# Spectral filter beside a gated MLP: background work tied one product later, and an eight-point butterfly in another order

## The chip, the cores and the metric

The kernel runs on one core of one Trainium2 chip. The metric is the time of one execution in device microseconds. Before the change it is 444.45 us, the median of three runs (443.97 to 444.93).

The core has five engines that run side by side, each through its own list of instructions in a fixed order: TensorE (PE), VectorE (DVE), ScalarE (ACT), GpSimd (POOL) and SyncE (SP), which starts the DMAs. An instruction waits at the head of its engine's list until the semaphores that it needs have been raised, and everything behind it waits too.

## The reference

The input is normalized by rows, and three things are summed: the input itself, a filter in the frequency domain (a two-dimensional FFT over sequence and features, a product with complex weights, the FFT back) and a gated MLP.

```python
# S, D, F = 2048, 448, 1792
def _A_ref(x, w_r, w_i):
    X = rfft2(x, axes=(-2, -1))
    X = X * (w_r + 1j * w_i)
    return irfft2(X, s=(S, D), axes=(-2, -1))

def _B_ref(x, W_gate, W_up, W_down):
    gate = jnp.einsum("bsd,df->bsf", x, W_gate)
    up = jnp.einsum("bsd,df->bsf", x, W_up)
    gate = gate * (gate > 0)
    return jnp.einsum("bsf,fd->bsd", gate * up, W_down)

x = A_x
xn = _layernorm(x, axis=-1)
return x + _A_ref(xn, A_w_r, A_w_i) + _B_ref(xn, B_W_gate, B_W_up, B_W_down)
```

## The kernel before

**The MLP is the foreground.** Every fp32 operand is split into two fp16 parts, a high and a low one, and each product is three matmuls (high by high, high by low, low by high). The 14 blocks of 128 hidden features stand in groups of 5, 5 and 4; the 2048 rows in four chunks of 512 (`CHUNKS`). A *gate/up unit* (`gu_unit`) multiplies one chunk by one block into two PSUM banks `gu`: 20 full matmuls of 512 columns in `gu_full`, and half matmuls in `gu_halves` that two units share. Its *product* (`gu_post`) is a chain over two engines: `gu_relu` on ACT (L887), `gu_times` on DVE (L891), `gu_hi` on ACT (L895), `gu_lo` on DVE (L899). The bank is free for a later unit when L891 has read it. A *down unit* (`dn_mm`, L923) multiplies 128 rows by a whole group into a bank that ACT presets with the running sum (`dn_seed`) and reads back (`dn_post`).

**The filter is the background.** It is a list `bg` of small steps, each with a cost in DVE time. Forward, for each of eight indices: `f_dft` (matmuls L417), an eight-point butterfly `f_a` and `f_b` on DVE over a tile `eo` with a scratch tile `bw`, a split (`f_hi` on ACT, `f_lo` on DVE L443), `f_sdft` (matmuls L450), then butterflies over sequence indices. In the middle the product with the weights. Inverse, for each index p of 0 to 7: `i_join` (DVE L678, L679) fills a tile `U[p]`; `i_swap` has SP copy its two partition halves crosswise into a tile `sw` by DMA; `i_pair` (L604, L605) adds them; `i_mix` runs the eight-point butterfly between `U[p]` and a scratch tile; `i_hi` (ACT L710) and `i_lo` (DVE, two L715) split the result into `vt`; `i_sdft` (matmuls L723) multiplies it into a bank `fx`; `i_pqhi` (ACT L729) and `i_pqlo` (DVE L732) split that into `wf` and free the bank; `i_ddft` (matmuls L753) makes 128-row blocks of output, in banks which ACT presets (L743) and reads back (L759), or, where a down unit holds the same rows, without a preset (`two_banks`) and with an addition on DVE (`i_acc`). U tiles, scratch tiles and weight tiles of the MLP share four buffers named `wst`, so their rows carry this name in a profile; `y` are the tiles of the butterflies over sequence indices, whose rotations are the pairs L458, L459 and L462, L463.

**What sets the order.** The opening (up to some 34 us) is written out by hand. Behind it, each unit issues its matmuls, then as many background steps as its share of DVE time pays for (`run_bg`, `room`), and then its product. The share is the same factor for all units, found so that the list ends `LASTGU` gate/up units before the last. A list scheduler then places all instructions on the engines by dependences, priorities and its own estimate of the time. `after(LAG)` binds every background step of a unit behind the last DVE and ACT instructions of an earlier product: `anchors` holds L891 and L887 of each unit so far (of a down unit its `dn_post`), and `LAG` says how many units back it reaches from the one just before.

The butterfly `eight_a`, `eight_b`, `turn` works on rows of 58 numbers, 16 rows to a tile (8 by real and imaginary part). Where an instruction reads or overwrites what an earlier DVE instruction touched, it carries a wait for that one.

Of the kernel before, what the change touches and what calls it, by code (L numbers as in the profile page):

```python
# [10 lines left out]
F32 = mybir.dt.float32  # L11
# [15 lines left out]
N2ORD = [0, 8, 4, 12, 2, 10, 6, 14, 1, 9, 5, 13, 3, 11, 7, 15]
CHUNKS = [0, 2, 1, 3]
# [12 lines left out]
"""  # L41
EXPMASK = 0x7F800000
EXPONE = float(1 << 23)
LASTGU = 9
SQ = 2.0 ** -16


# [96 lines left out]
def tile_gfnet_reglu(ctx: ExitStack, tc: tile.TileContext, x, xr, wgu, wd, wf, ident, c_fd, c_fm, c_im, c_row, c_id,  # L144
                     out):
    nc = tc.nc
    V, A, P, G = nc.vector, nc.scalar, nc.tensor, nc.gpsimd
# [4 lines left out]
    def mt(shape, dt, name, bufs=1):  # L152
        return main.tile(shape, dt, name=name, bufs=bufs)
# [65 lines left out]
    def load_xr(n2):  # L219
# [2 lines left out]
        xr_t[n2] = xr_b[n2].rearrange("p g c k -> p (g c k)")[:, 0:D]  # L222
        nc.sync.dma_start(xr_t[n2], xrv[:, n2, :])

    wst, wdst, fm_t, im_t, wf_t = {}, {}, {}, {}, {}

    def load_w(f, g, eng=nc.sync):
        if g == 0:
            t = mt([128, 2, 4, 128], F32, "wst", 4)
            wst[f, 0], wst[f, 1] = t[:, 0], t[:, 1]  # L230
        eng.dma_start(wst[f, g], wgu[f, :, g])

# [141 lines left out]

    def turn(o, a, b, u, v, sgn):

        o2 = o.rearrange("p l c k -> p (l c) k")
        x, y = slice(2 * a, 2 * b + 2, 2 * (b - a) + 1), slice(2 * b, 2 * a, 2 * (a - b) + 1)
        p, m = (OP.add, OP.subtract) if sgn > 0 else (OP.subtract, OP.add)
        V.tensor_tensor(o2[:, x], u, v[:, ::-1], op=p)  # L380
        V.tensor_tensor(o2[:, y], u, v[:, ::-1], op=m)

    def eight_b(X, w, s, sgn):

        turn(w, 4, 5, w[:, 3], w[:, 7], sgn)
        turn(w, 6, 7, w[:, 2], s[:, 2], sgn)
        V.tensor_tensor(X[:, 0], s[:, 0], s[:, 1], op=OP.add)
        V.tensor_tensor(X[:, 4], s[:, 0], s[:, 1], op=OP.subtract)
        turn(X, 2, 6, w[:, 0], w[:, 1], sgn)
        V.scalar_tensor_tensor(X[:, 1:8:6], w[:, 6:8], RT, w[:, 4:6], op0=OP.mult, op1=OP.add)  # L390
# [61 lines left out]
    def rotate(t, b, p, sgn):  # L452

        th = 2 * np.pi * p / 16
        c, s = float(np.cos(th)), float(np.sin(th)) * sgn
        if abs(c) >= abs(s) - 1e-9:
            k, f = s / c, c
            V.scalar_tensor_tensor(t[:, :, 0], b[:, :, 1], k, b[:, :, 0], op0=OP.mult, op1=OP.add)  # L458
            V.scalar_tensor_tensor(t[:, :, 1], b[:, :, 0], -k, b[:, :, 1], op0=OP.mult, op1=OP.add)  # L459
        else:  # L460
            k, f = c / s, s
            V.scalar_tensor_tensor(t[:, :, 0], b[:, :, 0], k, b[:, :, 1], op0=OP.mult, op1=OP.add)  # L462
            V.scalar_tensor_tensor(t[:, :, 1], b[:, :, 1], k, b[:, :, 0], op0=OP.mult, op1=OP.subtract)  # L463
        return f
# [195 lines left out]
    U = {}  # L660

    def i_join(p):

        u = U[p] = mt([128, 2, 4, 128], F32, "wst", 4).rearrange("p a b c -> p (a b c)")[:, 0:2 * XW].rearrange(
            "p (g c k) -> p g c k", g=NG, c=2)
        a, b = cur.pop(("i3", 0, p)), cur.pop(("i3", 1, p))
        o, d = (u[:, :, :, KC * i:KC * (i + 1)] for i in range(2))
        if p == 0:
            V.tensor_tensor(o, a, b, op=OP.add)
            V.tensor_tensor(d, a, b, op=OP.subtract)  # L670
        elif p == 4:
            for x, o1, o2 in ((o, OP.subtract, OP.add), (d, OP.add, OP.subtract)):
                V.tensor_tensor(x[:, :, 0], a[:, :, 0], b[:, :, 1], op=o1)
                V.tensor_tensor(x[:, :, 1], a[:, :, 1], b[:, :, 0], op=o2)
        else:
            t = free.pop(0)
            f = rotate(t, b, p, -1)
            V.scalar_tensor_tensor(o, t, f, a, op0=OP.mult, op1=OP.add)  # L678
            V.scalar_tensor_tensor(d, t, -f, a, op0=OP.mult, op1=OP.add)  # L679
            free.append(t)  # L680
        free.extend((a, b))
# [287 lines left out]
    def add(cost, fn, *a):  # L969
        bg.append((cost, PE_US.get(fn.__name__, 0.0), fn, a))  # L970
# [187 lines left out]
    for f in groups[1] + groups[2]:  # L1158
        s = first[f]
# [15 lines left out]
    for g, fs in enumerate(groups):  # L1175
        s = max(i for i in gus if i < first["dn", g])
# [192 lines left out]
```

## Time and profile before

| | |
|---|---|
| median of three runs | 444.45 us |
| profiled execution, whole | 444.21 us |
| its span, first to last instruction | 442.4 us |
| PE busy | 431.8 us, 3009 matmuls |
| DVE busy | 375.7 us, 922 instructions |
| ACT busy | 254.0 us |
| gate/up matmuls L852 | 1140, 255.8 us |
| down matmuls L923 | 624, 127.6 us |
| idle of DVE ahead of L891, ended by ACT's L887 | 18.4 us |
| idle of DVE ahead of L604, ended by the DMA of the swap | 5.1 us |

The profile comes from one execution with the hardware profiler. A row of a timeline has the start in us, the length, engine and line, the instruction, the tile written and the tiles read, shapes, how many instructions it merges, and in brackets how long the engine had been idle and what ended it. Instructions overlap at their ends, so the difference of two starts tells what one costs its engine. Engines other than PE may idle without cost, as long as PE doesn't wait for them.

### The profile page before, as it was taken

How to read it: one execution, taken by the hardware profiler on the slowest of the kernel's cores; microseconds unless marked ns; L12 is line 12 of the kernel's file. 1: busy time of each engine (PE TensorE's matmuls, PEld its weight loads, DVE VectorE, ACT ScalarE, POOL GpSimd, SP SyncE). 2: the span in 40 equal slices, each digit the busy share in tenths (PEclk: the TensorE clock that was granted, in tenths of full speed). 3: DMA queues.
4: the chain of work that ended last, by engine and by line, in shares of the span. 5: the costliest groups of instructions: out<-in, count | busy, mean ns of one | idle time of the engine just before them, and what ended most of it. 6: DMA issues, size and time to landing. Idle time of an engine off the chain costs nothing.

```text
span 442.4 us, 8132 instructions
## 1 busy us (share of the span) xinstructions
PE 431.8 (98%) x3009; PEld 209.9 (47%) x3009; DVE 375.7 (85%) x922; ACT 254.0 (57%) x515; POOL 39.7 (9%) x84
## 2 busy tenths in 40 slices
PE   6899999999999999999999999999999989999996
PEld 2543544454454444444444444444554544555544
DVE  5988798999988899999999998798989789974312
ACT  5888484587367837625425465664655653765530
POOL 2320030032300030000000041000000000000000
PEclk9999999999999999999999999999999999999999
DMA  7839995016000473522302100020201220120202
GB/s 251 296 92 243 382 296 103 2 32 77 3 0 2 144 219 120 164 85 65 107 1 85 42 1 1 2 85 1 89 10 56 77 74 17 63 76 7 105 22 83
DMA packets 38360, 39.66 MB, mean 90 GB/s; under 512 B 18592, under 2 KB 33216, under 8 KB 38320
## 3 DMA queue, kind: packets, MB, share of 16 engines
q1 hardware_dynamic: 38320, 39.14, 29.3%
q8 instruction: 23, 0.38, 0.4%
q14 instruction: 17, 0.14, 0.1%
HBM read 24.25 MB, written 3.67 MB: 63 GB/s over the span
## 4 chain that ended last, share of the span: by engine, by line
PE 76%; DVE 13%; DMA 6%; issue 1%; SPq 1%; ACT 0%; POOL 0%; DVEq 0%; ACTq 0%
PE gu L852 43%; PE dn L923 23%; DMA sw<-wst 3%; PE gu L859 3%; DMA wst<-in_wgu 2%; PE fx L450 2%; DVE vt L715 1%; PE fx L417 1%; DVE g L891 1%; PE fx L723 1%; DMA y<-in_xr 1%; DVE h L899 1%; PE dn L955 1%; DVE wst L604 1%; PE fx L753 1%
## 5 line engine op out<-in xcount | busy, mean ns | idle before, releaser
L852 PE MATMUL gu<-T,wt 128*128 128x512 f16 (+1 forms) x1140 | 255.8, 376 | 1.6 <-DVE g L891 1.2
L852 PEld LDWEIGHTS <-wt 128*128 128x128 f16 x1140 | 108.7, 98 | 132.4 <-issue 10.8
L923 PE MATMUL dn<-wdt,h 128*128 128x448 f16 x624 | 127.6, 353 | 0.0
L923 PEld LDWEIGHTS <-h 128*128 128x128 f16 x624 | 60.2, 98 | 57.0
L895 ACT ACTIVATE h<-g 128x512 f16<-128x512 f32 x56 | 34.9, 626 | 65.7 <-DVE g L891 65.6
L887 ACT ACTIVATE g<-gu 128x512 f32<-128x512 f32 x56 | 33.0, 589 | 38.5 <-PE gu L859 23.3
L891 DVE SCALAR_TENSOR_TENSOR g<-gu,g 128x512 f32<-128x512 f32 x56 | 38.4, 685 | 18.6 <-ACT g L887 18.4
L899 DVE TENSOR_TENSOR h<-g,h 128x512 f16<-128x512 f32 x56 | 38.3, 685 | 6.0 <-ACT h L895 6.0
L927 ACT ACTIVATE xy<-dn,dsc 128x448 f32<-128x448 f32 x44 | 27.6, 629 | 25.0 <-PE dn L923 24.9
L192 POOL PARTITION_ALL_REDUCE wm<-wm x15 | 16.0, 1072 | 155.8 <-ACT junk L189 155.8
L916 ACT ACTIVATE dn<-xy,dinv 128x448 f32<-128x448 f32 x44 | 27.6, 632 | 0.5
L805 DVE SCALAR_TENSOR_TENSOR wt<-wst,wsc,wt 128x512 f16<-128x512 f32 x28 | 20.6, 748 | 1.0 <-ACT wt L801 1.0
L801 ACT ACTIVATE wt<-wst,wsc 128x512 f16<-128x512 f32 x28 | 19.2, 713 | 1.8 <-DVE wsc L199 1.8
L189 ACT ACTIVATE junk<-wst 128x512 bf16<-128x512 f32 x28 | 17.4, 621 | 1.1 <-DMA wst<-in_wgu 0.9
L859 PE MATMUL gu<-T,wt 64*128 64x512 f16 x112 | 17.0, 381 | 0.1
L732 DVE SCALAR_TENSOR_TENSOR wf<-fx,wf 128x512 f16<-128x512 f32 x16 | 10.9, 688 | 4.9 <-ACT wf L729 4.9
L255 DVE BATCH_NORM_STATS2 bst<-y 128x6 f32<-128x448 f32 x16 | 9.6, 615 | 5.7 <-DMA y<-in_xr 5.7
L440 ACT ACTIVATE Xh<-eo 128x464 f16<-128x464 f32 x16 | 8.9, 596 | 8.7 <-DVE eo L391 8.7
L710 ACT ACTIVATE vt<-wst,fsc 128x928 f16<-128x928 f32 x8 | 8.8, 1097 | 8.6 <-DVE wst L391 6.1
L470 DVE TENSOR_TENSOR y<-y,y 128x464 f32<-128x464 f32 x21 | 13.4, 637 | 0.2
L471 DVE TENSOR_TENSOR y<-y,y 128x464 f32<-128x464 f32 x21 | 13.3, 636 | 0.0
L723 PEld LDWEIGHTS <-vt 128*128 128x128 f16 x192 | 11.4, 98 | 2.0 <-issue 0.4
(156 smaller groups left out, 506.8 us busy)
## 6 DMA issues: line engine op xcount, KB each, us to landing
wst<-in_wgu SPq DMA_DIRECT2D x28, 256.0 KB
wf<-in_wf SPq DMA_DIRECT2D x16, 232.0 KB
sw<-y SPq DMA_DIRECT2D x32, 114.2 KB
sw<-wst SPq DMA_DIRECT2D x16, 228.4 KB
y<-in_xr SPq DMA_DIRECT2D x16, 224.0 KB
xy<-in_x SPq DMA_DIRECT2D x16, 224.0 KB
out<-xy SPq DMA_DIRECT2D x15, 224.0 KB
wdst<-in_wd SPq DMA_DIRECT2D x14, 224.0 KB
```

What stands on the lines that cost most here:

```text
L189: A.activation(mt([128, 512], BF16, "junk")[:, 0:src.shape[-1]], src, AF.Square, scale=SQ, accum_out=acc)
L801: A.activation(w[:, 0:4, :], wst[f, g], AF.Copy, scale=wsc[f, g])
L805: V.scalar_tensor_tensor(w[:, 4:8, :], st, sc, w[:, 0:4, :], op0=OP.mult, op1=OP.subtract)
L852: last["P"] = P.matmul(hps[f, q][:, g, cs], wt[f, g][:, a, :], Tq[q][:, b, cs], start=(start and i == 0), stop=(stop and i == len(seq) - 1 ...
L859: m = P.matmul(hps[f, q][:, g, 0:512], wt[f, g][rows, 7, :], Tq[q][rows, b, :], start=start, stop=not start).ins
L887: last["A"] = A.activation(g1s[f, q], hps[f, q][:, 0, :], AF.Relu, scale=2.0 ** -22).ins
L891: last["V"] = V.scalar_tensor_tensor(g1, hps[f, q][:, 1, :], 2.0 ** -22, g1, op0=OP.mult, op1=OP.mult).ins
L895: A.activation(ht[f, q][:, 0, :], g1s[f, q], AF.Copy)
L899: V.tensor_tensor(h[:, 1, :], g1s.pop((f, q)), h[:, 0, :], op=OP.subtract)
L916: A.activation(dps[n2][:, 0:D], xy[n2], AF.Copy, scale=dinv[:, g:g + 1])
L923: last["P"] = P.matmul(dps[n2][:, 0:D], ht[f, q][:, a, js], wdt[f][:, b, :], start=False, stop=(f == fs[-1] and a == 1), skip_group_check= ...
L927: last["A"] = A.activation(xy[n2], dps[n2][:, 0:D], AF.Copy, scale=dsc[:, g:g + 1]).ins
```

## The change

Four things are changed; TensorE's, SP's and GpSimd's instructions are the same in number.

- `LAG` is 0 in place of 1: background steps of a unit are bound behind the product of the unit just before it, not the one before that.
- `LASTGU` is 11 in place of 9, so the background list ends two units earlier and each unit's share is larger. The costs of the forward butterfly's halves are 1.99 and 2.14 in place of 1.97 and 2.1.
- The tiles `wst` have 18 rows of 58 (1044 numbers) in place of 1024 numbers, and a butterfly takes the first 16 rows directly.
- The butterfly puts its second sums into rows 2, 4, 6 and its differences into rows 1, 3, 5 of the tile `F`, which leaves rows 0 to 2 of the scratch tile free for the next turn; `eight_b` takes the first sums ahead of the turns.

```diff
-LAG, AHEAD, RAMP = 1, 3, 6
+LAG, AHEAD, RAMP = 0, 3, 6
-LASTGU = 9
+LASTGU = 11
...
+    def wide():
+        return mt([128, 18, 2 * KC], F32, "wst", 4)
+
+    def eight_rows():
+        return wide()[:, 0:2 * NG].rearrange("p (g c) k -> p g c k", c=2)
...
-            t = mt([128, 2, 4, 128], F32, "wst", 4)
+            t = wide().rearrange("p a k -> p (a k)")[:, 0:1024].rearrange("p (g a b) -> p g a b", g=2, a=4)
...
-        V.tensor_tensor(s, w[:, 0:3], w[:, 4:7], op=OP.add)
-        V.tensor_tensor(w[:, 0:3], w[:, 0:3], w[:, 4:7], op=OP.subtract)
+        V.tensor_tensor(F[:, 2:7:2], w[:, 0:3], w[:, 4:7], op=OP.add)
+        V.tensor_tensor(F[:, 1:6:2], w[:, 0:3], w[:, 4:7], op=OP.subtract)
...
+        V.tensor_tensor(F[:, 0], F[:, 2], F[:, 4], op=OP.add)
+        V.tensor_tensor(F[:, 4], F[:, 2], F[:, 4], op=OP.subtract)
         turn(w, 4, 5, w[:, 3], w[:, 7], sgn)
-        turn(w, 6, 7, w[:, 2], s[:, 2], sgn)
-        V.tensor_tensor(X[:, 0], s[:, 0], s[:, 1], op=OP.add)
-        V.tensor_tensor(X[:, 4], s[:, 0], s[:, 1], op=OP.subtract)
-        turn(X, 2, 6, w[:, 0], w[:, 1], sgn)
-        V.scalar_tensor_tensor(X[:, 1:8:6], w[:, 6:8], RT, w[:, 4:6], op0=OP.mult, op1=OP.add)
-        V.scalar_tensor_tensor(X[:, 5:2:-2], w[:, 6:8], -RT, w[:, 4:6], op0=OP.mult, op1=OP.add)
+        turn(w, 0, 1, F[:, 5], F[:, 6], sgn)
+        turn(F, 2, 6, F[:, 1], F[:, 3], sgn)
+        V.scalar_tensor_tensor(F[:, 1:8:6], w[:, 0:2], RT, w[:, 4:6], op0=OP.mult, op1=OP.add)
+        V.scalar_tensor_tensor(F[:, 5:2:-2], w[:, 0:2], -RT, w[:, 4:6], op0=OP.mult, op1=OP.add)
...
-            state["mix"] = mt([128, 2, 4, 128], F32, "wst", 4).rearrange("p a b c -> p (a b c)")[:, 0:2 * XW].rearrange(
-                "p (g c k) -> p g c k", g=NG, c=2)
-            eight_a(u, state["mix"], u[:, 1:4])
+            state["mix"] = eight_rows()
+            eight_a(u, state["mix"])
...
-        add(1.97, f_a, a)
-        add(2.1, f_b, a)
+        add(1.99, f_a, a)
+        add(2.14, f_b, a)
```

The first two constants and the scheduler move instructions all over the program, so what stands where is shown at three places. In the changed kernel's rows a line number is 4 to 6 higher for the same instruction (L887 is L891, L891 is L895, L732 is L736, L380 is L386).

First the butterfly itself, on DVE: the first forward one, in tiles `eo` and `bw`, with the waits that its rows carry (`DVE` for a wait on an earlier DVE row). Before:

```order
L372 TENSOR_TENSOR eo<-bw 128x348 [waits DVE_49]
L373 TENSOR_TENSOR bw<-bw 128x348 [waits DVE_49]
L387 TENSOR_TENSOR eo<-eo 128x116
L388 TENSOR_TENSOR eo<-eo 128x116
L271 RECIPROCAL rs<-rs 128x4 [waits Activation_49]
L380 TENSOR_TENSOR bw<-bw 128x2x58 [waits DVE_49]
L381 TENSOR_TENSOR bw<-bw 128x2x58
L380 TENSOR_TENSOR eo<-bw 128x2x58 [waits DVE_49]
L381 TENSOR_TENSOR eo<-bw 128x2x58
```

After the change, the same place:

```order
L378 TENSOR_TENSOR eo<-bw 128x3x116 [waits DVE_49]
L379 TENSOR_TENSOR eo<-bw 128x3x116
L391 TENSOR_TENSOR eo<-eo 128x116 [waits DVE_49]
L386 TENSOR_TENSOR bw<-bw 128x2x58 [waits DVE_49]
L387 TENSOR_TENSOR bw<-bw 128x2x58
L386 TENSOR_TENSOR bw<-eo 128x2x58
L392 TENSOR_TENSOR eo<-eo 128x116 [waits DVE_49]
L387 TENSOR_TENSOR bw<-eo 128x2x58
L386 TENSOR_TENSOR eo<-eo 128x2x58 [waits DVE_49]
```

The second difference no longer waits for the row directly ahead, and most other waits are for rows two or more back. (In the inverse butterflies before, nearly each of these rows waited for the one ahead.)

Second, DVE where the last split of inverse index 3 stands (L732, `wf`, of which the second frees the bank that ACT presets for the matmuls L753). Before:

```order
L891 SCALAR_TENSOR_TENSOR g1_4537<-gu_4469,g1_4537 128x512
L604 TENSOR_TENSOR wst_4527<-wst_4527,sw0_2361 128x8x58
L605 TENSOR_TENSOR wst_4527<-wst_4527,sw0_2361 128x8x58
L380 TENSOR_TENSOR wst_4624<-wst_4624 128x2x58
L732 SCALAR_TENSOR_TENSOR wf_4348<-fx_4322,wf_4348 128x512
L715 SCALAR_TENSOR_TENSOR vt_2359<-wst_4169,fsc_88,vt_2359 128x16x29 x2
L732 SCALAR_TENSOR_TENSOR wf_4350<-fx_4335,wf_4350 128x512
L381 TENSOR_TENSOR wst_4624<-wst_4624 128x2x58
L899 TENSOR_TENSOR h_4540<-g1_4537,h_4540 128x512
L380 TENSOR_TENSOR wst_4624<-wst_4624,wst_4352 128x2x58
L891 SCALAR_TENSOR_TENSOR g1_4639<-gu_4490,g1_4639 128x512
```

After, from the pairing to the second split:

```order
L610 TENSOR_TENSOR wst_4500<-wst_4500,sw0_2270 128x8x58
L611 TENSOR_TENSOR wst_4500<-wst_4500,sw0_2270 128x8x58
L903 TENSOR_TENSOR h_4617<-g1_4614,h_4617 128x512
L378 TENSOR_TENSOR wst_4314<-wst_4569 128x3x116
L379 TENSOR_TENSOR wst_4314<-wst_4569 128x3x116
L736 SCALAR_TENSOR_TENSOR wf_4310<-fx_4284,wf_4310 128x512
L391 TENSOR_TENSOR wst_4314<-wst_4314 128x116
L719 SCALAR_TENSOR_TENSOR vt_2268<-wst_4137,fsc_88,vt_2268 128x16x29 x2
L386 TENSOR_TENSOR wst_4569<-wst_4569 128x2x58
L387 TENSOR_TENSOR wst_4569<-wst_4569 128x2x58
L386 TENSOR_TENSOR wst_4569<-wst_4314 128x2x58
L736 SCALAR_TENSOR_TENSOR wf_4312<-fx_4297,wf_4312 128x512
```

Between the pairing and the second split stand a low part of the MLP and six butterfly rows more; the next product (L895) follows seven rows behind it.

Third, ACT in the forward transform, at the first relu behind the opening (`g1_1038`). Before:

```order
L320 ACTIVATE tt1_102<-y15_81,rs_964 128x448
L320 ACTIVATE tt2_103<-y14_80,rs_964 128x448
L320 ACTIVATE tt3_104<-y0_66,rs_964 128x448
L927 ACTIVATE xy_61<-dn_847,dsc_91 128x448
L887 ACTIVATE g1_1038<-gu_979 128x512
L493 ACTIVATE y11_77<-fx_822 128x464
```

After:

```order
L931 ACTIVATE xy_61<-dn_847,dsc_91 128x448
L324 ACTIVATE y15_81<-y9_75,rs_964 128x448
L324 ACTIVATE y14_80<-y17_83,rs_964 128x448
L324 ACTIVATE y0_66<-y8_74,rs_964 128x448
L920 ACTIVATE dn_1433<-xy_61,dinv_92 128x448
L499 ACTIVATE y11_77<-fx_822 128x464
L326 ACTIVATE tt0_101<-y12_78,rs_964 128x448
L326 ACTIVATE tt1_102<-y15_81,rs_964 128x448
L446 ACTIVATE Xh_864<-eo_818 128x464
L446 ACTIVATE Xh_866<-eo_818 128x464
L326 ACTIVATE tt2_103<-y14_80,rs_964 128x448
L891 ACTIVATE g1_1038<-gu_979 128x512
```

The relu, which stood directly behind the read-back of the down unit (L927), now stands behind three normalizations, a preset, the evacuation L499 and five more rows.

More of the change, by code (lines that the diff above doesn't have):

```diff
@@ L363, in tile_gfnet_reglu, with eight_a @@
     RT = float(np.sqrt(0.5))
-    def eight_a(F, w, s):
+    def eight_a(F, w):
         f, p = (t.rearrange("p (h s) c k -> p h s (c k)", h=2) for t in (F[:, 0:8], w[:, 0:8]))
@@ L381, in turn, with eight_b @@
         V.tensor_tensor(o2[:, y], u, v[:, ::-1], op=m)
-    def eight_b(X, w, s, sgn):
+    def eight_b(F, w, sgn):
+        V.tensor_tensor(F[:, 0], F[:, 2], F[:, 4], op=OP.add)
+        V.tensor_tensor(F[:, 4], F[:, 2], F[:, 4], op=OP.subtract)
         turn(w, 4, 5, w[:, 3], w[:, 7], sgn)
-        turn(w, 6, 7, w[:, 2], s[:, 2], sgn)
-        V.tensor_tensor(X[:, 0], s[:, 0], s[:, 1], op=OP.add)
-        V.tensor_tensor(X[:, 4], s[:, 0], s[:, 1], op=OP.subtract)
-        turn(X, 2, 6, w[:, 0], w[:, 1], sgn)
-        V.scalar_tensor_tensor(X[:, 1:8:6], w[:, 6:8], RT, w[:, 4:6], op0=OP.mult, op1=OP.add)
-        V.scalar_tensor_tensor(X[:, 5:2:-2], w[:, 6:8], -RT, w[:, 4:6], op0=OP.mult, op1=OP.add)
+        turn(w, 0, 1, F[:, 5], F[:, 6], sgn)
+        turn(F, 2, 6, F[:, 1], F[:, 3], sgn)
+        V.scalar_tensor_tensor(F[:, 1:8:6], w[:, 0:2], RT, w[:, 4:6], op0=OP.mult, op1=OP.add)
+        V.scalar_tensor_tensor(F[:, 5:2:-2], w[:, 0:2], -RT, w[:, 4:6], op0=OP.mult, op1=OP.add)
     def chained(m, prev):
@@ L428, in f_a @@
         w = state["bw"] = ft([128, NG, 2, 2 * KC], F32, "bw")
-        eight_a(Fq[a], w, Fq[a][:, 1:4])
+        eight_a(Fq[a], w)
     def f_b(a):
-        eight_b(Fq[a], state["bw"], Fq[a][:, 1:4], 1)
+        eight_b(Fq[a], state["bw"], 1)
     def f_part(a, n2):
@@ L662, in i_join @@
     def i_join(p):
-        u = U[p] = mt([128, 2, 4, 128], F32, "wst", 4).rearrange("p a b c -> p (a b c)")[:, 0:2 * XW].rearrange(
-            "p (g c k) -> p g c k", g=NG, c=2)
+        u = U[p] = eight_rows()
         a, b = cur.pop(("i3", 0, p)), cur.pop(("i3", 1, p))
@@ L697, in i_mix @@
         if half == 0:
-            state["mix"] = mt([128, 2, 4, 128], F32, "wst", 4).rearrange("p a b c -> p (a b c)")[:, 0:2 * XW].rearrange(
-                "p (g c k) -> p g c k", g=NG, c=2)
-            eight_a(u, state["mix"], u[:, 1:4])
+            state["mix"] = eight_rows()
+            eight_a(u, state["mix"])
         else:
-            eight_b(u, state["mix"], u[:, 1:4], -1)
+            eight_b(u, state["mix"], -1)
     def i_sides(p):
```

## Prediction

> **What bounds the kernel now.** I read the page's first part, then TensorE's order in time, then the in-order queues of VectorE (DVE) and ScalarE (ACT) where TensorE stops.
>
> ```profile
> span 442.4 us, 8132 instructions
> PE 431.8 (98%) x3009; PEld 209.9 (47%) x3009; DVE 375.7 (85%) x922; ACT 254.0 (57%) x515; POOL 39.7 (9%) x84
> PE 76%; DVE 13%; DMA 6%; issue 1%; SPq 1%; ACT 0%; POOL 0%; DVEq 0%; ACTq 0%
> ```
>
> TensorE is busy for 431.8 of 442.4 us, and neither program gives it other work (3009 matmuls in both). A gain can come only from places where it stands still behind the warm-up; a loss comes from any new one. DVE holds 13% of the chain that ended last, so somewhere it sets the time. That place is the inverse transform:
>
> ```profile
> 312.00:371.00 59.00, 57.38 (x527) 29.89 (x525) 53.05 (x125) 33.30 (x57) 0.00 (x0) 1.00 0.18 58
> 371.00:437.00 66.00, 66.00 (x585) 35.28 (x582) 35.53 (x74) 33.48 (x57) 0.00 (x0) 1.00 0.14 48
> ...
> 305.36 0.60 PE L859 MATMUL gu<-T,wt 64*128 64x512 f16 x4
> 305.89 4.49 PE L852 MATMUL gu<-T,wt 128*128 128x512 f16 x20
> ...
> 362.75 0.54 PE L923 MATMUL dn<-wdt,h 128*128 128x448 f16 x2
> 364.48 4.48 PE L852 MATMUL gu<-T,wt 128*128 128x512 f16 x20 [1.19 <-DVE g L891]
> 368.79 0.73 PE L923 MATMUL dn<-wdt,h 128*128 128x448 f16 x3
> 369.84 0.80 PE L753 MATMUL fx<-idc_t,wf 64*128 64x56 f16 x48 [0.31 <-ACT fx L743]
> 370.74 0.61 PE L859 MATMUL gu<-T,wt 64*128 64x512 f16 x4
> ```
>
> The first two rows are stretches: length, then the busy time of PE, weight loads, DVE, ACT and GpSimd. DVE works 53 of 59 us in the first, 35.5 of 66 in the second. In the others, columns are start and length. By starts, 20 gate/up matmuls take 4.31 us (364.48 to 368.79), 0.216 each; I take 0.19 for a down matmul. So TensorE waits 1.73 - 2 x 0.19 = 1.35 us ahead of 364.48 for a product on DVE (L891), 1.05 - 3 x 0.19 = 0.48 us ahead of 369.84 for the preset of a bank by ACT (L743), and about 0.1 ahead of 370.74. Together 1.9 us: everything that the change could win in the middle of the kernel. Why DVE is late there:
>
> ```profile
> 306.69 0.69 DVE L891 SCALAR_TENSOR_TENSOR g<-gu,g 128x512 f32<-128x512 f32 x1 [1.72 <-ACT g L887]
> 309.02 1.31 DVE L715 SCALAR_TENSOR_TENSOR vt<-wst,fsc,vt 128x464 f16<-128x464 f32 x2
> 310.24 0.69 DVE L899 TENSOR_TENSOR h<-g,h 128x512 f16<-128x512 f32 x1
> ...
> 313.65 0.40 DVE L462 SCALAR_TENSOR_TENSOR y<-y 128x232 f32<-128x232 f32 x1
> 313.96 0.40 DVE L463 SCALAR_TENSOR_TENSOR y<-y 128x232 f32<-128x232 f32 x1
> ...
> 322.49 0.64 DVE L604 TENSOR_TENSOR wst<-wst,sw 128x464 f32<-128x464 f32 x1 [1.81 <-DMA sw<-wst]
> ...
> 331.38 0.27 DVE L387 TENSOR_TENSOR wst<-wst 128x116 f32<-128x116 f32 x1
> 331.57 0.27 DVE L388 TENSOR_TENSOR wst<-wst 128x116 f32<-128x116 f32 x1
> ...
> 347.54 0.64 DVE L679 SCALAR_TENSOR_TENSOR wst<-y,y 128x464 f32<-128x464 f32 x1
> 348.10 0.40 DVE L390 SCALAR_TENSOR_TENSOR wst<-wst 128x232 f32<-128x232 f32 x1
> ...
> 354.15 0.64 DVE L604 TENSOR_TENSOR wst<-wst,sw 128x464 f32<-128x464 f32 x1 [2.37 <-DMA sw<-wst]
> ...
> 357.85 0.64 DVE L679 SCALAR_TENSOR_TENSOR wst<-y,y 128x464 f32<-128x464 f32 x1
> 358.40 0.28 DVE L380 TENSOR_TENSOR wst<-wst 128x116 f32<-128x116 f32 x1
> 358.71 0.28 DVE L381 TENSOR_TENSOR wst<-wst 128x116 f32<-128x116 f32 x1
> 359.02 0.28 DVE L380 TENSOR_TENSOR wst<-wst 128x116 f32<-128x116 f32 x1
> ...
> 365.31 0.64 DVE L604 TENSOR_TENSOR wst<-wst,sw 128x464 f32<-128x464 f32 x1 [0.88 <-DMA sw<-wst]
> ...
> 368.43 0.68 DVE L732 SCALAR_TENSOR_TENSOR wf<-fx,wf 128x512 f16<-128x512 f32 x1
> 369.03 0.27 DVE L381 TENSOR_TENSOR wst<-wst 128x116 f32<-128x116 f32 x1
> ```
>
> From the end of the first low part (L715, ended by 310.24) to the end of the second L732 of index 3 (369.03) DVE needs 58.8 us. Of this, 5.06 us (1.81 + 2.37 + 0.88) are waits for the swap of partition halves by DMA, which lands 6.05 us (348.10 to 354.15) to 6.9 us (358.40 to 365.31) after the join that feeds it. And the same 116-element row costs 0.19 us from start to start when free (331.38), 0.31 us when it must wait for the row ahead (358.40 onward): 0.12 us for each such wait. The order has 26 of them in this stretch, 3.1 us.
>
> **The change, step by step.** I count on both programs' orders, in rows from the first low part to the second L732 of index 3, and price with the rows above. (The changed kernel's line numbers are 4 to 6 higher; I keep the old ones.)
>
> Butterflies: same rows and elements, and waits on the row directly ahead fall from 113 to 89 on DVE in the whole program, from 26 to 6 in this stretch: 20 x 0.12 = -2.4 us on DVE. Rows two apart for the outputs of L372/L373 I cost at nothing: the spacing goes with the elements (116 in 0.19, 464 in 0.56 from 347.54 to 348.10), and the first butterfly rows are strided already. Outside the inverse DVE's cover is large, and the four gained waits there win nothing. The Trainium skill ("VectorE: DVE Perf Modes", section on the drain that can't be avoided) says a semaphore after each instruction costs nothing extra, since the pipe is flushed anyway. By that the term would be 0 and the sum 2.4 us worse; the trace's 0.19 against 0.31 speaks against it, though a wait on an older row is free here too.
>
> Rows moved into the stretch: 129 rows in place of 121. Four more rotations (0.31 each by 313.65 and 313.96), one more L899 (0.60 by 310.24 to 310.84), two more weight rows L838 and two more turns, one sum less (0.19 each). For L838 (448 elements) I take 0.60 from L899 with 512, an upper bound; a lower is 0.55. Together 1.24 + 0.60 + 1.20 + 0.38 - 0.19 = +3.2 us.
>
> Swap waits: five joins stand in the stretch. With 6.05 to 6.9 us of latency, and the DVE rows that now stand between join and pairing: first 6.1 us, wait 0 to 0.3; second 3.5 us, 2.5; third 10 us, none; fourth 4.8 us and two loads ahead of it on SP's queue, 1.3 to 2; fifth 4.7 us, 1.35. That is 5.2 to 6.1; I take 5.8, +0.7 against 5.06. Faster butterflies are partly given back here, since the latency doesn't shrink. Bounds: none at all (-5.06) and 5 x 2.5.
>
> So 58.8 + 3.2 - 2.4 + 0.7 = 60.3 us.
>
> Start of the stretch: now counted from the four half matmuls at 305.36, 4.9 us (310.24). Before, ACT's relu (L887) comes right behind them and the high part (L710) after it. In the new order L710 stands ahead of L887, and L710 waits for the last butterfly step on DVE:
>
> ```profile
> 306.06 0.60 ACT L887 ACTIVATE g<-gu 128x512 f32<-128x512 f32 x1 [2.61 <-PE gu L859]
> 306.56 1.09 ACT L710 ACTIVATE vt<-wst,fsc 128x928 f16<-128x928 f32 x1
> ```
>
> If L710 is over by then, the stretch starts at 1.33 + 0.6 + 1.22 = 3.2 us (306.69 less 305.36, L891, two L715). If it still waits, its 1.0 us and DVE's remaining rows go in front, 6.3 us. DVE's rows from the preceding product to that last step make 5.4 us, and three butterfly rows stand ahead of that product, so I take 5.6: +0.7.
>
> End of the stretch: from 369.03 to 369.84 is 0.8 us to the matmuls L753. TensorE's own work from 305.36 to there is 64.48 - 1.83 = 62.65 us, now two down matmuls less, 62.25. The new wait ahead of L753 is 5.6 + 60.3 + 0.8 - 62.25 = 4.4 us in all, some of it earlier, at the second L723 group. Before it is 1.83: +2.6 us. Behind L753 stand the half matmuls that need a bank from L891, which the new order puts seven rows (a turn, a sum, two joins, two turns, itself: 0.19 + 0.19 + 1.1 + 0.38 + 0.69 = 2.55 us) behind the second L732, while L743 and L753 need 0.64 + 0.8 = 1.5: 1.05 us against 0.1, so +0.9 us.
>
> Forward: the first relu behind the opening was early on ACT; it now stands behind five rows more.
>
> ```profile
> 61.39 0.61 PE L859 MATMUL gu<-T,wt 64*128 64x512 f16 x4
> ...
> 71.47 0.82 PE L417 MATMUL fx<-fd_t,T 64*128 64x58 f16 x48
> ...
> 62.38 1.78 ACT L320 ACTIVATE tt<-y,rs 128x448 f16<-128x448 f32 x3
> 64.06 0.62 ACT L927 ACTIVATE xy<-dn,dsc 128x448 f32<-128x448 f32 x1
> 64.58 0.59 ACT L887 ACTIVATE g<-gu 128x512 f32<-128x512 f32 x1
> ...
> 66.59 0.68 DVE L891 SCALAR_TENSOR_TENSOR g<-gu,g 128x512 f32<-128x512 f32 x1
> 68.28 1.18 DVE L443 TENSOR_TENSOR Xh<-eo,Xh 128x464 f16<-128x464 f32 x2
> ```
>
> With T the start of the half matmuls: the down matmuls ahead of them end at T - 1.2; ACT does L927 (0.52), three normalizations and a seed (0.56 each) and L493 (0.6), T + 2.15; DVE then does two sums (1.1), three low parts (0.8 each), two L443 (1.1) and L891 (0.7): T + 7.45. TensorE is there at T + 0.54 + 20 x 0.216 + 6 x 0.19 + 0.76 = T + 6.8. So +0.65 us; bounds 0 (as before) and 1.5 if the normalizations come late.
>
> Background tied later (LAG) and a fuller share per unit (LASTGU) issue nothing of their own. One more pair of the last transforms goes without presets: four additions more on DVE and two presets and two evictions less on ACT, after 371, where DVE idles 30 of 66 us; cover enough. SP's and GpSimd's other moves (loads, weight maxima) feed rows several units away and nobody on TensorE waits for them before. The last inverse transform comes behind the last gate/up product and the final sums end less bunched; the tail after the last matmul I leave as it is.
>
> Sum: +2.6 + 0.9 + 0.65 = +4.15; the price of L838 being an upper bound, +4.0. The profiled execution took 444.21 us (span 442.4 and 1.8 around it); the median is 0.24 above it. 444.45 + 4.0 = **448.4 us** (span 446.4).
>
> **Rivals.** *DVE catches up (faster):* the 20 cheaper rows let DVE reach the second L732 in time. It decides when 4.4 us less stand on DVE, which the swap waits alone could give, if they fell from 5.8 to 1.4 as the DMA overlaps better. Then the 1.9 us vanish: 442.5. For it speaks that DVE idles 6 of 59 us here; against it that the swaps chain on each other.
>
> *One late row traded for another (same):* the start term is 3.2 in place of 5.6, and the forward wait is covered. Then 4.15 - 2.4 - 0.65 = 1.1, and with swap waits at the lower bound 0.5: about 444.9.
>
> *The clock falls:* nothing here cost TensorE its full rate after the opening, but the opening does:
>
> ```profile
> 1.49 5.93 PE L1194 MATMUL dn<-bw 128*128 128x512 f16 x19 [1.49 <-POOL bw L1251]
> ```
>
> 19 matmuls in 5.93 us are 0.312 each against 0.216, 1.8 us lost. If the 4.4 us fall into one wait and TensorE starts cold again, 448.4 + 1.8 = 450.2. The Trainium skill ("TensorE: Matmul & The Clock Gate", Part 1) puts the fall at an idle window of some 3.4 us; the longest wait in this trace behind the opening, 1.35 us, doesn't test it.
>
> *Waits on DVE are free after all:* the -2.4 is 0, then 450.8; the spacing rows contradict it. That is the rule weighed above, of the Trainium skill ("VectorE: DVE Perf Modes").
>
> **How the numbers follow.** About 0.2% is what a measurement of this kernel tells from no change. Forecast (446 to 450) 0.64; DVE catches up 0.13; trade 0.13, mostly within 0.2%; clock 0.06; free waits 0.04. That makes faster 0.15, same 0.10, slower 0.75. The range goes from 444.0, which leaves out the faster case, to 450.6, which takes in the clock and most of the start term's upper bound.
>
> **What would show it.** Right: no wait of L753 or L859 near 370 is shorter than now, L381-like rows of the inverse at 0.19 start to start instead of 0.31, relu L887 behind L710 at the first inverse index, a wait of TensorE for L891 of about 0.6 us near 70. Wrong: TensorE's rows run on without an idle number between 311 and 375 us. The forecast falls if swaps land in under 5 us after their join, or if ACT reaches L710 before the product's matmuls end.

## The result, and the profile after

The changed kernel takes 452.24 us (median of 6 runs, 451.43 to 453.18), the kernel before 444.27 in the same session: a ratio of 1.0183 (95% interval 1.0173 to 1.0193), or +8.0 us. Forecast were +4.0 and a range that ended at 450.6. The direction was right, the size half of what came.

From the page of the changed kernel: its span, TensorE's line, the clock granted to TensorE in 40 slices of 11.3 us, and the engines' shares of the chain of waits that ended last.

```profile
span 451.4 us, 8147 instructions
PE 435.2 (96%) x3009; PEld 211.1 (47%) x3009; DVE 375.1 (83%) x926; ACT 251.7 (56%) x512; POOL 35.7 (8%) x84
PEclk9999999999999999999999999999999996999999
PE 64%; DVE 18%; DMA 10%; SPq 3%; issue 2%; ACT 2%; POOL 0%; DVEq 0%; ACTq 0%
```

The span grew by 9.0 us, in the profiled execution 453.16 us against 444.21. DVE's busy time is the same within 0.6 us. The chain holds more DVE (18% against 13%), more DMA (10% against 6%) and SP's queue (3% against 1%), and one slice of the clock shows a 6 that was not there before. Where TensorE stands still (start, length, then idle time and what ended it):

```profile
69.15 0.82 PE L423 MATMUL fx<-fd_t,T 64*128 64x58 f16 x48
70.46 4.48 PE L856 MATMUL gu<-T,wt 128*128 128x512 f16 x20 [0.48 <-DVE g L895]
...
306.44 0.60 PE L863 MATMUL gu<-T,wt 64*128 64x512 f16 x4
...
329.17 0.38 PE L856 MATMUL gu<-T,wt 128*128 128x512 f16 x1
330.88 1.35 PE L727 MATMUL fx<-im,vt 128*128 128x128 f16 x20 [1.33 <-DVE vt L719]
...
333.79 0.92 PE L927 MATMUL dn<-wdt,h 128*128 128x448 f16 x4
335.09 4.48 PE L856 MATMUL gu<-T,wt 128*128 128x512 f16 x20 [0.38 <-DVE g L895]
...
370.20 0.35 PE L927 MATMUL dn<-wdt,h 128*128 128x448 f16 x1
375.25 1.30 PE L757 MATMUL fx<-idc_t,wf 64*128 64x56 f16 x48 [4.70 <-ACT fx L747]
377.04 1.04 PE L863 MATMUL gu<-T,wt 64*128 64x512 f16 x4 [0.48 <-DVE g L895]
378.01 5.83 PE L856 MATMUL gu<-T,wt 128*128 128x512 f16 x18
383.67 1.50 PE L727 MATMUL fx<-im,vt 128*128 128x128 f16 x24
```

Counted as in the prediction (starts, less the matmuls between them at 0.216 and 0.19), TensorE waits 1.49 us ahead of 330.88, 0.54 ahead of 335.09 and 4.86 ahead of 375.25. Then 18 gate/up matmuls take 5.66 us by their starts (378.01 to 383.67), 0.31 each in place of 0.216: for most of them TensorE is at half clock. In windows that start and end where the granted clock changes, PE's busy time stands first behind the length and the clock ahead of the last two columns:

```profile
371.39:374.80 3.41, 0.00 (x0) 0.00 (x0) 3.41 (x10) 1.43 (x3) 0.00 (x0) 1.00 0.00 0
374.80:378.21 3.41, 2.47 (x53) 1.43 (x53) 3.38 (x10) 2.10 (x5) 0.00 (x0) 0.50 0.06 12
378.21:381.63 3.42, 3.42 (x9) 1.22 (x8) 3.35 (x12) 0.98 (x2) 0.00 (x0) 0.50 0.39 130
```

A window of 3.41 us in which TensorE did nothing is followed by 6.83 us at half clock. Why the product was so late is seen in DVE's waits for the swap between the first low part and the second split of index 3 (in all, times, longest), and in its rows there:

```profile
DVE wst L610 <- DMA sw<-wst: 8.0, 4, 2.9
```

```profile
322.37 0.65 DVE L610 TENSOR_TENSOR wst<-wst,sw 128x464 f32<-128x464 f32 x1 [0.61 <-DMA sw<-wst]
...
327.91 0.64 DVE L610 TENSOR_TENSOR wst<-wst,sw 128x464 f32<-128x464 f32 x1 [1.95 <-DMA sw<-wst]
...
349.44 0.64 DVE L684 SCALAR_TENSOR_TENSOR wst<-y,y 128x464 f32<-128x464 f32 x1
...
357.70 0.64 DVE L610 TENSOR_TENSOR wst<-wst,sw 128x464 f32<-128x464 f32 x1 [2.89 <-DMA sw<-wst]
...
360.83 0.64 DVE L684 SCALAR_TENSOR_TENSOR wst<-y,y 128x464 f32<-128x464 f32 x1
...
368.69 0.64 DVE L610 TENSOR_TENSOR wst<-wst,sw 128x464 f32<-128x464 f32 x1 [2.51 <-DMA sw<-wst]
```

From the end of its join to its pairing, index 5 takes 7.6 us (350.08 to 357.70) and index 6 takes 7.2 (361.47 to 368.69). SP's queue in the changed kernel shows what stands around these two swaps (L693, L694):

```profile
350.23 0.99 SPq L588 DMA_DIRECT2D im<-in_c_im  x2
351.31 0.54 SPq L691 DMA_DIRECT2D wst<-row  x1
351.90 0.79 SPq L693 DMA_DIRECT2D sw<-wst  x1
352.74 0.76 SPq L694 DMA_DIRECT2D sw<-wst  x1
353.61 0.42 SPq L943 DMA_DIRECT2D out<-xy  x1
...
363.00 0.76 SPq L694 DMA_DIRECT2D sw<-wst  x1
363.87 0.41 SPq L943 DMA_DIRECT2D out<-xy  x1
364.39 1.98 SPq L588 DMA_DIRECT2D im<-in_c_im  x2
```

Two loads stand between the join of index 5 and its swap, which starts 1.8 us behind the join's end; a store, and for index 6 two loads, stand right behind it.

### The profile page after: what moved, and what is told of

Read it like the earlier page. It is cut to its first block, busy times and chain, and to the rows that moved or that the text cites. A ratio compares the mean times of both kernels' runs of the same rounds, so it can differ in the third digit from the quotient of the medians.

```text
span 451.4 us, 8147 instructions
## 1 busy us (share of the span) xinstructions
PE 435.2 (96%) x3009; PEld 211.1 (47%) x3009; DVE 375.1 (83%) x926; ACT 251.7 (56%) x512; POOL 35.7 (8%) x84
## 4 chain that ended last, share of the span: by engine, by line
PE 64%; DVE 18%; DMA 10%; SPq 3%; issue 2%; ACT 2%; POOL 0%; DVEq 0%; ACTq 0%
PE gu L856 36%; PE dn L927 19%; DMA sw<-wst 4%; DMA xy<-in_x 3%; PE gu L863 2%; PE fx L456 2%; DVE g L895 2%; DVE wt L809 1%; DVE h L903 1%; DVE vt L719 1%; DMA y<-in_xr 1%; PE fx L727 1%; DMA wst<-in_wgu 1%; PE dn L959 1%; DVE wf L736 1%
## 5 line engine op out<-in xcount | busy, mean ns | idle before, releaser
L856 PE MATMUL gu<-T,wt 128*128 128x512 f16 (+1 forms) x1140 | 256.2, 377 | 1.3 <-DVE g L895 0.9
L856 PEld LDWEIGHTS <-wt 128*128 128x128 f16 x1140 | 109.3, 98 | 134.0 <-issue 13.2
L927 PE MATMUL dn<-wdt,h 128*128 128x448 f16 x624 | 127.4, 353 | 0.0
L927 PEld LDWEIGHTS <-h 128*128 128x128 f16 x624 | 60.2, 98 | 57.4 <-issue 0.7
L891 ACT ACTIVATE g<-gu 128x512 f32<-128x512 f32 x56 | 33.0, 590 | 34.3 <-PE gu L863 25.7
L895 DVE SCALAR_TENSOR_TENSOR g<-gu,g 128x512 f32<-128x512 f32 x56 | 38.4, 686 | 14.6 <-ACT g L891 14.5
L192 POOL PARTITION_ALL_REDUCE wm<-wm x15 | 11.4, 757 | 157.4 <-ACT junk L189 157.4
L863 PE MATMUL gu<-T,wt 64*128 64x512 f16 x112 | 17.5, 389 | 0.5 <-DVE g L895 0.5
L736 DVE SCALAR_TENSOR_TENSOR wf<-fx,wf 128x512 f16<-128x512 f32 x16 | 10.9, 688 | 7.9 <-ACT wf L733 7.7
L733 ACT ACTIVATE wf<-fx 128x512 f16<-128x512 f32 x16 | 9.4, 588 | 9.0 <-PE fx L727 8.9
L476 DVE TENSOR_TENSOR y<-y,y 128x464 f32<-128x464 f32 x21 | 13.4, 637 | 0.5 <-DMA row<-y 0.3
L727 PE MATMUL fx<-im,vt 128*128 128x128 f16 x192 | 12.4, 219 | 1.3 <-DVE vt L719 1.3
L610 DVE TENSOR_TENSOR wst<-wst,sw 128x464 f32<-128x464 f32 x8 | 5.1, 641 | 10.2 <-DMA sw<-wst 10.2
```

The lines of the kernel that those rows point to most:

```text
L856: last["P"] = P.matmul(hps[f, q][:, g, cs], wt[f, g][:, a, :], Tq[q][:, b, cs], start=(start and i == 0), stop=(stop and i == len(seq) - 1 ...
L863: m = P.matmul(hps[f, q][:, g, 0:512], wt[f, g][rows, 7, :], Tq[q][rows, b, :], start=start, stop=not start).ins
L891: last["A"] = A.activation(g1s[f, q], hps[f, q][:, 0, :], AF.Relu, scale=2.0 ** -22).ins
L895: last["V"] = V.scalar_tensor_tensor(g1, hps[f, q][:, 1, :], 2.0 ** -22, g1, op0=OP.mult, op1=OP.mult).ins
L927: last["P"] = P.matmul(dps[n2][:, 0:D], ht[f, q][:, a, js], wdt[f][:, b, :], start=False, stop=(f == fs[-1] and a == 1), skip_group_check= ...
```

## The experiments

"Before" is timed beside each set of runs (443.8 to 444.2 us), and ratios are against that.

**LASTGU back to 9, all else as changed.**

```diff
-LASTGU = 11
+LASTGU = 9
```

> The changed kernel with LASTGU back at 9, LAG still 0, the new butterfly and costs kept. Theory S (the fuller share per unit of LASTGU 11 moves background rows into the inverse stretch and lines the swaps up behind each other): the waits of TensorE at 329 and 370 us go, no stretch at half clock, 443.0 to 445.5 us. Rival L (the binding one product later, LAG 0, makes DVE late): still 449 to 453 us. Rival B (the new butterfly's rows are placed worse): 449 us or more too.

443.7 us, ratio 0.9994 (0.9985 to 1.0004). The whole loss is gone, with LAG 0 and the new butterfly still there. TensorE's one wait behind 40 us is the forward one. In the whole inverse DVE waits for swaps:

```profile
DVE wst L610 <- DMA sw<-wst: 3.6, 2, 2.3
```

That is 3.6 us, against 10.2 in the changed kernel (8.0 in the stretch and 2.2 ahead of it). One more pairing waits 2.1 us for another DMA of the same step (`wst<-row`), which this number leaves out. Theories L and B fall as sole causes.

**LAG back to 1, all else as changed.**

```diff
-LAG, AHEAD, RAMP = 0, 3, 6
+LAG, AHEAD, RAMP = 1, 3, 6
```

> The changed kernel with LAG back at 1, LASTGU still 11, the new butterfly and costs kept. Theory S: still slower than before, 446 to 452 us, with a wait of TensorE of 2 us or more between 325 and 375 us. Rival L: 443.5 to 445 us.

447.17 us, ratio 1.0069 (1.0048 to 1.009). A good half of the loss goes. In the profiled execution, of 448.08 us, swap waits are 7.0 us, TensorE's longest wait is 3.0 us, and the clock falls, for one window:

```profile
367.94 1.30 PE L757 MATMUL fx<-idc_t,wf 64*128 64x56 f16 x48 [3.00 <-ACT fx L747]
```

```profile
364.57:367.98 3.41, 0.41 (x5) 0.13 (x5) 3.41 (x8) 2.35 (x4) 0.00 (x0) 1.00 0.00 0
367.98:371.39 3.41, 3.41 (x54) 1.96 (x54) 3.41 (x7) 1.12 (x2) 0.00 (x0) 0.50 0.20 61
```

It does not fall in every execution: two of the four kept a mean clock of 1.000 (445.83 and 447.10 us), and they too are slower than the kernel before.

**The kernel before with LASTGU 11 alone.**

```diff
-LASTGU = 9
+LASTGU = 11
```

> The kernel before with LASTGU 11 alone. Theory S: slower, 446 to 452 us. Rivals L and B: 444 to 445 us, no change.

444.27 us, ratio 1.0004 (0.9992 to 1.0015): no change, a miss for S as I had put it. With the old butterfly, a fuller share per unit is not enough. Swap waits fell to 2.5 us here, and TensorE's one wait of 1.29 us (ahead of a down unit) took the place of the 1.9 us of before.

**The changed kernel with two stores later.** The stores of blocks 0 and 8 are tied behind that of block 2; the lists of TensorE, DVE and ACT stay.

```diff
+        if n2 in stored and n2 in (0, 8):
+            held.append(n2)
+        elif n2 in stored:
+            ahead = nc.sync.dma_start(ov[:, n2, cs], xy[n2][:, cs]).ins
+            while held:
+                k = held.pop()
+                with tc.issue_after(ahead):
+                    nc.sync.dma_start(ov[:, k], xy[k])
```

> The changed kernel in which the stores of output blocks 0 and 8, which SP issues right behind the fourth and fifth swap (at 353.6 and 363.9 us), are tied behind the store of block 2 near 388 us; PE, DVE and ACT keep their orders. Theory S with the clock (the wait near 370 us is a chain of swaps, and the half clock behind it comes from the wait's length): the swaps' second halves land in about 4.3 us in place of 4.84 and 5.56, the wait of 4.86 us shrinks to 3.2 to 3.8; if that is short enough the clock stays full and the time is 446.5 to 448 us, if not 450.5 to 451 us. If the stores don't matter to the swaps: 452 us as before.

451.18 us, ratio 1.0159 (1.0142 to 1.0176). Swap waits fall by 1.5 us (to 8.7), TensorE's long wait by 1.3 (idle 3.37 in place of 4.70), the span by 1.5 (to 449.9). The clock still falls, for the same 6.83 us, and the time is 0.2 us above what was expected for that case. The waits for the two swaps fell from 2.89 to 2.32 us and from 2.51 to 1.77: here a store right behind a swap delayed it by 0.6 to 0.7 us, and TensorE paid that nearly in full.

**The kernel before with LAG 0 alone**, and **with LAG 0 and LASTGU 11.**

```diff
-LAG, AHEAD, RAMP = 1, 3, 6
+LAG, AHEAD, RAMP = 0, 3, 6
...
-LASTGU = 9
+LASTGU = 11
```

(The first run has only the upper pair.)

> The kernel before with LAG 0 alone (LASTGU 9, old butterfly). Theory C (the loss comes from LAG 0 and LASTGU 11 together, each harmless alone): same as before within 0.3%, 443 to 445, TensorE's longest wait behind the opening under 1.5 us. Theory L2 (LAG 0 is harmful wherever the butterfly is slow, and the first experiment escaped only by the faster butterfly): 445.5 to 448, with a wait of 2 us or more behind index 2 or 3 of the inverse.

> The kernel before with LAG 0 and LASTGU 11 (old butterfly, old costs). Theory C (the two numbers together bring the loss, the butterfly not): slower than before, 447 to 453, waits of TensorE at the inverse transform of 5 us or more in sum. Rival N (the new butterfly's order is needed for the loss as well): 443.5 to 446. If one single wait reaches 3 us or more, a stretch of half clock follows it; if the waits stay under 3 us each, none does, and the time is the sum of the waits.

444.81 us, ratio 1.0012 (1.0003 to 1.0021), for LAG 0 alone; 450.13, ratio 1.0138 (1.0119 to 1.0157), for both. C holds: each number is nearly harmless alone, the two together bring +6 us with the old butterfly. Swap waits are 5.5 us with LAG 0 alone and 8.6 with both. There TensorE's longest idle times are 1.74 and 2.85 us, and the second already drops the clock in the profiled execution:

```profile
371.39 1.01 PE L852 MATMUL gu<-T,wt 128*128 128x512 f16 x2 [2.85 <-DVE g L891]
```

```profile
367.77:371.18 3.41, 0.77 (x5) 0.29 (x3) 3.41 (x8) 1.05 (x2) 0.00 (x0) 1.00 0.03 10
371.18:374.59 3.41, 3.20 (x53) 1.70 (x53) 3.41 (x9) 1.30 (x3) 0.00 (x0) 0.50 0.02 5
```

So the bound that I had set there for the clock, 3 us, was too high for this execution. Of the other three, two show a lower mean clock too (0.996 and 0.992), and one kept 1.000 (449.72 us).

**The kernel before with the new butterfly alone** (the whole diff of the butterfly and of the rows of 58), and **with the two new cost numbers too.**

```diff
-        add(1.97, f_a, a)
-        add(2.1, f_b, a)
+        add(1.99, f_a, a)
+        add(2.14, f_b, a)
```

> The kernel before with the new butterfly and the rows of 58 alone (LAG 1, LASTGU 9, old costs). The butterfly saves DVE 0.12 us for each wait on the row directly ahead that goes away, but TensorE's waits behind the opening are only 1.9 us in all. Theory D (the waits are DVE's lateness): part or all of the 1.9 us goes, 442.5 to 444.0. Rival F (the swap's landing sets the pace, so that a faster butterfly only waits longer for it): within 0.2% of before, 443.5 to 444.6, and the waits for the swap grow by what the rows lose.

> The kernel before with the new butterfly, the rows of 58 and the two new cost numbers (LAG 1, LASTGU 9). The cost numbers shift the bounds of the units' shares a little. Theory D: 442.0 to 443.5, faster than before, and no wait of TensorE over 0.7 us behind 40 us. Rival F: 443.5 to 444.6.

443.25 us, ratio 0.9981 (0.9973 to 0.999), and 442.69, ratio 0.9967 (0.9955 to 0.998): faster than before and than the changed kernel. D holds. With the butterfly alone swap waits are 2.9 us and TensorE's longest wait is 0.71; with the cost numbers no wait of TensorE over 0.4 us is left behind 40 us, swap waits are 2.0 us, and the chain that ended last is TensorE almost alone:

```profile
PE 91%; DVE 5%; DMA 1%; issue 1%; SPq 0%; POOL 0%; ACT 0%; DVEq 0%; ACTq 0%
```

All eight in one table (us; in brackets the inverse transform's swap waits in the profile):

| | LAG 1, LASTGU 9 | LAG 0, LASTGU 9 | LAG 1, LASTGU 11 | LAG 0, LASTGU 11 |
|---|---|---|---|---|
| old butterfly and costs | 444.2 (5.1) | 444.81 (5.5) | 444.27 (2.5) | 450.13 (8.6) |
| new butterfly and costs | 442.69 (2.0) | 443.7 (3.6) | 447.17 (7.0) | 452.24 (10.2) |

In this table every kernel with 7 us of swap waits or more takes 447 us or more, and none with less does. The sum is no rule, though. With LAG 0 and LASTGU 9 one pairing waits 2.1 us more for the DMA `wst<-row`, which with the old butterfly makes 7.6 us, and yet TensorE's longest wait is 1.29 us; and the kernel with a clear queue, below, takes 447.74 us with 5.8 by the same view.

The table also shows that the edits don't add up one by one. LASTGU 11 alone changes nothing with the old butterfly and costs 4.5 us with the new one (442.69 to 447.17). The new butterfly with its costs gains 1.1 to 1.5 us at LASTGU 9 and loses 2.1 to 2.9 at LASTGU 11.

**The changed kernel with a clear queue.** The tables of the inverse transform (`im`) get 12 buffers and are loaded ahead of it, and the two stores stand later as above. TensorE's, DVE's and ACT's lists are those of the changed kernel.

```diff
-        im_t[n2] = it([128, 2, 128], F16, "im", 3)
+        im_t[n2] = it([128, 2, 128], F16, "im", 12)
...
-            both(0.0, load_im, p + 2) if p >= 0 else [both(0.0, load_im, k) for k in (0, 1)]
+            (both(0.0, load_im, p + 6) if p < 2 else 0) if p >= 0 else [both(0.0, load_im, k) for k in range(6)]
```

> The changed kernel with SP's queue cleared around the inverse swaps: the tables of the inverse transform are loaded ahead of it (12 buffers in place of 3) and the stores of blocks 0 and 8 stand behind that of block 2. The lists of TensorE, DVE and ACT are the changed kernel's. Theory Q (what stands on SP's queue between and behind the swaps makes them late): the wait for the swap of index 5 falls to about 1.3 us, that of index 6 to about 1.4, all swap waits from 10.2 to about 7.3; TensorE's wait ahead of L757 falls to about 2 us, under what dropped the clock so far (2.9 to 4.9 us), so the clock stays and the time is 446 to 447.5. Rival K (the fall of the clock does not come from that wait): half clock at the same place, 449 or more. Rival R (the queue does not matter, only the rows between join and pairing): 450.5 to 451.5 as with the late stores alone.

447.74 us, ratio 1.0098 (1.0068 to 1.0129): 0.2 us above Q's range (the half matmuls L863 now wait 0.99 us in place of 0.48), below K and R. Its waits for swaps and its TensorE rows:

```profile
DVE wst L610 <- DMA sw<-wst: 5.8, 4, 2.2
```

```profile
370.06 0.35 PE L927 MATMUL dn<-wdt,h 128*128 128x448 f16 x1
372.08 0.80 PE L757 MATMUL fx<-idc_t,wf 64*128 64x56 f16 x48 [1.67 <-ACT fx L747]
373.87 0.61 PE L863 MATMUL gu<-T,wt 64*128 64x512 f16 x4 [0.99 <-DVE g L895]
374.41 4.06 PE L856 MATMUL gu<-T,wt 128*128 128x512 f16 x18
378.31 1.50 PE L727 MATMUL fx<-im,vt 128*128 128x128 f16 x24
```

Swap waits fell by 4.4 us; of these the pairing of index 6 still idles 1.2 us, which this view no longer puts down to the DMA, so 3.2 us is the safer number (7.0 left, 7.3 expected). TensorE's long wait fell from 4.86 to 1.83, and the clock stays at 1.00 in this execution; in one of the other three, of 450.51 us, the mean clock was 0.988. The pairing of index 5 now comes 5.9 us behind its join, that of index 6 too: 1.7 and 1.3 us less than with the loads and the stores around them. The loads alone, with the stores where they were, were not run. The rows also give the clock's price, since both kernels run the same list here: 48 L757 take 0.80 us in place of 1.30, four L863 0.54 by their starts in place of 0.97, 18 L856 3.90 in place of 5.66. That is 2.69 us. About 0.5 of it stands in place of the wait ahead of L863 (0.99 us at full clock, 0.48 at half), so from the start of L757 to the start of L727 half clock costs 2.19 us net (8.42 against 6.23).

**The best version with a clear queue.** The same edits on the kernel of 442.69.

> The kernel of the earlier run with the new butterfly and the new cost numbers alone (LAG 1, LASTGU 9), with SP's queue cleared in the same way. Theory D: there the waits for the swap are only 2.0 us and TensorE has no wait that they cause, so the cleared queue wins nothing: 442.2 to 443.2, within 0.2% of that run. If it is under 442.0, swaps still cost time there.

442.9 us, ratio 0.9972 (0.9963 to 0.9981), not to be told from that kernel: where swaps make nobody wait, a clear queue wins nothing.

## Why the prediction was right in direction and short by half

**Right, with numbers.** The start of the stretch: relu L887, now L891, came behind L710, now L714, and the first low part was over 5.63 us behind the half matmuls (306.44 to 312.07), forecast 5.6. ACT's and DVE's rows there:

```profile
308.63 1.10 ACT L714 ACTIVATE vt<-wst,fsc 128x928 f16<-128x928 f32 x1 [4.09 <-DVE wst L397]
309.64 0.58 ACT L891 ACTIVATE g<-gu 128x512 f32<-128x512 f32 x1
```

```profile
310.25 0.69 DVE L895 SCALAR_TENSOR_TENSOR g<-gu,g 128x512 f32<-128x512 f32 x1 [0.87 <-ACT g L891]
...
312.07 0.40 DVE L464 SCALAR_TENSOR_TENSOR y<-y 128x232 f32<-128x232 f32 x1
```

The butterfly's rows stand 0.19 apart when they don't wait for the row ahead and 0.31 when they do:

```profile
362.14 0.28 DVE L387 TENSOR_TENSOR wst<-wst 128x116 f32<-128x116 f32 x1
362.33 0.28 DVE L392 TENSOR_TENSOR wst<-wst 128x116 f32<-128x116 f32 x1
362.64 0.28 DVE L386 TENSOR_TENSOR wst<-wst 128x116 f32<-128x116 f32 x1
```

The two row terms (+3.2 moved, -2.4 for the butterfly) add to +0.8. DVE's stretch took 62.4 us (312.07 to 374.44, the end of the second split of index 3), 3.6 more than before; swap waits gave 2.9 of it (7.96 in place of 5.06), which leaves 0.7 for the rows; only their sum is measured here, not each of the two. The forward wait was forecast at 0.65; it is 0.56 (70.46 less 69.15, less 0.75 for 48 L417, which take that from 71.47 to 72.22 in the kernel before).

**The step that failed: the swap waits.** The prediction took "5.2 to 6.1; I take 5.8". They were 0.61 + 1.95 + 2.89 + 2.51 = 7.96, 2.2 us more. This is most of what TensorE's lateness missed (5.06 us, forecast 2.6). The rows between join and pairing were counted rightly: for indices 5 and 6 I had 4.8 and 4.7 us, and the trace has 4.7 each (7.6 - 2.9, 7.2 - 2.5). The latency, from the join to the landing of its swap, was wrong. For index 6 I used the short one, 6.05 us. But the row with the same neighbours was quoted in the prediction: 358.40 to 365.31, 6.9 us, in the kernel before, where SP's queue shows a store and two loads behind the swap too:

```profile
348.95 0.79 SPq L688 DMA_DIRECT2D sw<-wst  x1
...
359.23 0.76 SPq L688 DMA_DIRECT2D sw<-wst  x1
...
360.88 0.41 SPq L939 DMA_DIRECT2D out<-xy  x1
361.39 1.96 SPq L582 DMA_DIRECT2D im<-in_c_im  x2
```

It took 7.2 in the changed kernel. For index 5 I counted the two loads ahead but at 0.1 to 0.7 us; the swap started 1.1 us later behind its join than before (1.8 against 0.8), and the store behind it cost 0.6 more by the experiment with the late stores. With the clear queue the stretch idles 4.8 us at pairings (1.2 of them not put down to the DMA) and takes 59.1 us, near the 60.3 of the forecast, and so does the time: 447.74 against 448.4.

**The second step: the clock at nothing.** With DVE 2.2 us later, the single wait ahead of L757 became 4.86 us, and the clock fell. The forecast's sum has no term for that. The prediction had it as a rival, at a chance of 0.06 and at 1.8 us, the price in the opening; the rows say 2.69, or 2.19 net. With 1.83 us of wait, in the profile of the clear queue, it doesn't fall. The prediction put 4.4 us "in all, some of it earlier", and only in that rival asked what happens "if the 4.4 us fall into one wait"; it never worked out how long the longest single wait would be.

**The sum, as it came** (span): lateness ahead of L757 and earlier 6.89 - 1.83 = +5.06 (forecast +2.6); half matmuls 0.48 - 0.1 = +0.38 (+0.9; the slow L757 hid some); forward +0.56 (+0.65); clock +2.69 (0). Together +8.7 of the measured +9.0.

**Which edit.** With LAG 1 and LASTGU 9 the butterfly alone is worth -0.9 us, with its cost numbers -1.5. DVE did catch up there, as the first rival has it (442.5 forecast, 442.69 measured), but only with the background placed as before; at LASTGU 11 the same butterfly costs time. LAG 0 and LASTGU 11 together cost 6 us with the old butterfly and 9.5 with the new one. The prediction said that the two issue nothing of their own; that is so, and they decide the time by the order. What in the planner makes LASTGU 11, with LAG 0 or with the new butterfly, line the swaps up was not tried and stays open. Shown is that the swap waits come with it, and that without the loads and stores around the swaps about half of the loss goes (8.0 us become 3.7).

## What to carry to other kernels

Where a transfer stands in a chain between two rows of an engine, take its latency from a row with the same neighbours on its queue, those behind it included; the queue's order is part of the price. When a sum of lateness comes out, split it into single waits, since a long wait of TensorE can cost its length and the clock behind it. Two numbers that change next to nothing each can cost 6 us together, and a local gain (here the butterfly, 1.5 us) can turn into a loss under other planner numbers: try such edits in pairs, not only one by one.

## What was not expected of the hardware

In the inverse transform the clock fell behind windows of 3.41 us in which TensorE had worked 0.00, 0.41 and 0.77 us (the rows above), thus already with an idle time of 2.85 us. It stayed up there through idle times of 1.29, 1.67 and 1.74 us. A single long wait isn't needed, though. In the profile of the kernel before with LASTGU 11 the clock also fell in the opening, at 11.12 us for one window: in the window ahead of it (7.71 to 11.12) TensorE had worked 1.49 us, and the idle times that reach into it were 1.30 and 1.19 us. On the grid that the clock's own changes set, the emptiest windows that kept it held 1.67 us of work (330.22 to 333.63, the kernel before with LAG 0 and LASTGU 11) and 1.75 us (369.00 to 372.42, the clear queue). So the work within a window orders all these cases, and the longest idle time doesn't. Where between 1.49 and 1.67 us the bound lies was not tried.

The Trainium skill ("TensorE: Matmul & The Clock Gate", Part 1) says that the clock is halved after at least one idle window of about 3.4 us, and that these windows run freely. The length and the grid agree with the traces: in the changed kernel the clock rises at 6.16 us and falls at 374.80, which is 108 windows of 3.413 us. If idle means without any work, the traces don't agree: 1.49 us of work didn't save the clock.

The same kernel can keep its clock in one execution and lose it in the next (the mean clocks above). A grid that runs freely, so that the same wait falls into one window or is cut by two, would explain it; that was not tried.

Half clock lasted one window where TensorE was busy for 3.41 or 3.20 us of it, and two where it was busy for 2.47 (changed kernel) or 2.90 (late stores); there the end of the long wait and a second wait of 0.48 us fell into the first. That a second short wait right behind a long one doubles the time at half clock fits all four cases, but was not tried by itself.

A butterfly row of 0.28 us that waits for the row directly ahead starts 0.31 us behind it, and one that doesn't 0.19 us: 0.12 us for each such wait. The Trainium skill ("VectorE: DVE Perf Modes", section on the drain that can't be avoided) says that a semaphore after each instruction costs nothing extra. For these short rows the traces don't agree. The new butterfly, which has fewer such waits, made the kernel 0.9 us faster by itself; that all of it comes from these waits was not shown apart.
